# Transposes of q, k and x on TensorE, or by DMA between SBUF tiles: attention with a window and sinks, then an MLP, on one core

## The chip, the cores and the metric

The kernel runs on one core of one Trainium2 chip. The core has five engines that run side by side and wait for each other through semaphores: PE (TensorE, matrix products; PEld is its loading of weights), DVE (VectorE), ACT (ScalarE), POOL (GpSimd) and SP (SyncE). SP issues DMAs only; POOL and ACT issue DMAs too. DMAs move data between device memory and SBUF, or within SBUF, on 16 DMA engines that all queues share. The metric is the time of one execution on the device in microseconds; lower is better. Profiled executions carry a trace of every instruction.

## What is computed

Attention over 4 batches and 8 heads, 768 tokens each, head size 64. A token sees the 4 first tokens of its sequence (sinks) and the 128 tokens up to itself (window). The result of all heads, 512 numbers for a token, goes through an MLP with 2048 hidden units.

```python
def _attn_ref(q, k, v, n_sink, window) -> np.ndarray:
    B, H, S, D = q.shape
    scale = 1.0 / np.sqrt(D)
    scores = scale * np.matmul(q, k.transpose(0, 1, 3, 2))
    ...
    is_sink = pos[None, :] < int(n_sink)
    rel = pos[:, None] - pos[None, :]
    in_window = (rel >= 0) & (rel < int(window))
    keep = is_sink | in_window
    scores = np.where(keep, scores, -1000000000.0)
    scores = scores - np.max(scores, axis=-1, keepdims=True)
    a = np.exp(scores)
    a = a / (np.sum(a, axis=-1, keepdims=True) + 1e-09)
    return np.matmul(a, v).astype(np.float32)

def _moe_ref(x, w_in, w_out) -> np.ndarray:
    h = x @ w_in
    g = h * (1.0 / (1.0 + np.exp(-1.702 * h)))
    return (g @ w_out).astype(np.float32)
```

Inputs and output are float32; inside, the kernel works on float16 with float32 sums.

## The kernel before

**Tiling.** The 3072 tokens (4 batches x 768) are cut into 12 blocks of 256, three to a batch; `k` is the block, `r` its place in the batch, `j` the half of 128 tokens. The 8 heads are handled as 4 pairs, `p`. A block goes through these steps:

- Load (`load`, `load_rounded`, lines 425 to 481): POOL issues DMAs that bring q and k of the block into `qk16` and v into `v16`, rounding to float16 on the way: four DMAs for q and k and four for v. Blocks 0 and 1 load q, k or both through SP and ACT in float32 and round on an engine (`load_cast`). `qk16` and `v16` are rings of four buffers, so the loads of block k+4 wait for the last reader of block k.
- Transpose q and k (`front`, line 550, for blocks 0 to 3; `halves_qk`, line 604, from block 4): the scores need the head dimension on the partitions. PE transposes through PSUM and DVE or ACT copies the result to `qkT` (ring of three). From block 4 these are 32 transposes of 64 x 128 (line 618), put in behind the score matmuls of pairs 2 and 3 of the block before, into two PSUM banks.
- Sinks (`front`, lines 572 to 595): at r = 0, the transposed keys of the 4 sink tokens go to `ks16`; at r = 1 and 2 a matmul gives the scores against them (line 585) and ACT their exponentials (`ats`). The values of the sinks go to `vs16` through small DMAs on SP (line 474).
- Scores (`scores`, line 695), their exponentials on ACT (line 724, `at`) and a multiplication with `mask` on DVE (lines 738 and 742).
- Attention times values (`back`, lines 770 and 775), then DVE divides by the sum: a reciprocal (line 790) and a product (line 792) that writes `xn`, with the tokens on the partitions (ring of three).
- Transpose x (`back`, line 803, for blocks 0 to 2 and 11; `halves_x`, line 642, for blocks 3 to 10): 16 transposes of 64 x 128 a block, put in behind the score matmuls of pairs 0 and 1 of the next block, then two copies to `xT` (ring of three).
- First layer (`mm1`, line 843): 16 groups of four matmuls of 128 x 128 by 256 columns, tanh on ACT (line 857), and a DVE instruction (line 859) that writes `gT`.
- Second layer (`mm2_seven`, line 920, for blocks 1 to 11): seven products of half-size matrices in place of eight, with sums on DVE (lines 890 and 947); results go to `osb`, and SP issues the output DMAs (line 996). Block 0 takes `mm2` (line 1021).

**Order of the tokens.** In `qk16`, `v16` and all that follows, the tokens of a block do not stand in their natural order but with even and odd tokens apart, which the loads arrange by their address patterns. `mask` is made for that order on POOL (line 335), the sinks are found at the matching places, and the outputs are written as `paired` rows, two DMAs for each half of a block (lines 993 to 998).

**Order of the work.** The order of the instructions on each engine is fixed when the program is built. `Plan` (line 55) receives operations with an engine, a duration, a latency, their dependencies and a due time (`prio`, from `nominal(k, slot)` with a period of 16.6 us for a block); it plays them through in time, one engine at a time, taking the operation that can start first, and among those that can start within 20 ns the one with the lowest `prio`. What it decides is the order; the chip's own times then decide the waits. A DMA is an operation with the issue's duration and the transfer's share of the DMA engines; its end adds a fixed time and a lag (line 176). PSUM is eight banks that an operation acquires and a later one releases; the score operations with transposes behind them acquire six (line 710).

```python
            elif isinstance(lat, tuple):
                dma_free = max(s + (2400 if e == "POOL" else 2000), dma_free) + lat[0]
                o.end = dma_free + (lag(dma_free) if o.kind != "out" else 500)
```

PE works on several blocks at once: between the attention of one block and its first layer stand the first and second layer of the blocks before it. SP's instructions are a queue of their own: an output DMA that waits for `osb` holds what stands behind it.

Of the kernel before, what the change touches and what calls it, by code (L numbers as in the profile page):

```python
# [10 lines left out]
FP16 = mybir.dt.float16  # L11
AF = mybir.ActivationFunctionType
ALU = mybir.AluOpType

P = 128
D = 64
# [188 lines left out]
def kernel(  # L205
# [28 lines left out]

    EARLY = {1: 4, 2: 5, 3: 0}
    HALVES_FROM, HALVES_X_FROM = 4, 3
    V1_BEHIND = None

    SPLIT_TO = 1
# [13 lines left out]

    ident = pool.tile([P, P], FP16, name="ident")
    mask = pool.tile([P, 4 * P], FP16, name="mask")
    bias = pool.tile([P, 4 * P], FP16, name="bias")
    dummy = pool.tile([P, 8], FP16, name="dummy")
    zero = pool.tile([P, P], FP16, name="zero")
# [30 lines left out]
    def f16(o, i=0):  # L289
        return bank[o.banks[i]][:, 0:256].bitcast(FP16)  # L290
# [47 lines left out]
    def keep_sinks():  # L338
# [8 lines left out]
    o_bias = op("DVE", 310, 420, lambda: nc.vector.tensor_scalar(  # L347
        out=bias, in0=mask, scalar1=-1.0, scalar2=-OUT, op0=ALU.add, op1=ALU.mult), [o_mask], prio=MASK_AT, kind="mask")

    def ones():  # L350
        for t in v16:
            nc.vector.memset(t[:, :, :, D : D + 1], 1.0)
# [68 lines left out]
    def load_rounded(k, es, war):  # L421

        b, r = divmod(k, R)
        t0 = r * TB
        prio = load_at(f"a{k}")
        c16 = qk16[k % RQ].rearrange("p (i e h d) -> p i e h d", i=2, e=2, h=H)
        n = 2 if k <= SPLIT_TO else 1
        for c in range(n):
            hs = slice(c * H // n, (c + 1) * H // n)
            for e in es:  # L430
                src = (q, k_ap)[e]
                for i in range(2):
                    def f(e=e, i=i, hs=hs, src=src):
                        nc.gpsimd.dma_start(  # L434
                            c16[:, i, e, hs], src[b, hs, t0 : t0 + TB].rearrange("h (p i) d -> i p h d", i=2)[i]
                        )
                    o = op("POOL", ISSUE if n > 1 else ISSUE + 190, (QK_NS / n,), f, war,
                           prio=prio + 0.1 * c + 0.02 * (2 * e + i), kind="load")
                    loads.append(o)
                    for p in range(c * NP // n, (c + 1) * NP // n):  # L440
                        o_cqk.setdefault((k, p), []).append(o)

    def load(k):
        b, r = divmod(k, R)
        t0 = r * TB
        war = reuse("qk16", k % RQ)
        if k < max(ROUNDED_FROM):
            load_cast(k, [e for e in range(2) if k < ROUNDED_FROM[e]], war)
        load_rounded(k, [e for e in range(2) if k >= ROUNDED_FROM[e]], war)
        w16 = v16[k % RV]  # L450

        war = reuse("v16", k % RV) + ([o_ks[0, V1_BEHIND]] if k == 1 and V1_BEHIND is not None else [])

        o_cv[k] = []
        for j in range(2):
            for i in range(2):
                src = v[b, :, t0 + P * j : t0 + P * j + P].rearrange("h (a i) d -> i a h d", i=2)[i]
                o = op("POOL", ISSUE, (430 if k < 2 else V_NS,), lambda i=i, j=j, src=src: nc.gpsimd.dma_start(  # L458
                    w16[64 * i : 64 * i + 64, j, :, 0:D], src), war + [o_ones],
                       prio=load_at(f"v{k}"), kind="load")  # L460
                if not loads:
                    o.behind = o_mask0
                loads.append(o)
                o_cv[k].append(o)
        if r == 0:

            o_vs[b] = []
            for t in range(2):
                for i in range(2):
                    to = vs16[64 * t + 32 * i : 64 * t + 32 * i + 2, b, :, i]  # L470
                    fr = w16[64 * t : 64 * t + 2, 0, i::2, 0:E]
                    deps = [o_cv[k][t], o_vs0[b]]
                    if b:
                        o = op("SP", 450, (20,), lambda to=to, fr=fr: nc.sync.dma_start(to, fr), deps,
                               prio=nominal(k - 1, 0), kind="vs")
                    else:

                        o = plan.any(pick({"POOL": (400, 500), "DVE": (220, 320), "ACT": (420, 540)}, VS_ON),
                                     lambda eng, to=to, fr=fr: copy(eng, to, fr), deps, prio=VS_AT, kind="ks")
                    o_vs[b].append(o)  # L480
                    uses("v16", k % RV, o)
# [59 lines left out]
    def front(k, p):  # L541
# [5 lines left out]
        T = qkT[k % RKT]  # L547
        c16 = qk16[k % RQ].rearrange("p (i e h d) -> p i e h d", i=2, e=2, h=H)

        if k < HALVES_FROM:  # L550
            def tp():
                ps = f16(o_tp).rearrange("d (e j i p) -> d e j i p", e=2, j=2, i=2)
                for i in range(2):
                    for e in range(2):
                        nc.tensor.transpose(  # L555
                            ps[:, e, :, i, :], c16[:, i, e, 2 * p : 2 * p + 2].rearrange("s h d -> s (h d)"), ident
                        )

            if p == 0:
                o_T["war", k] = reuse("qkT", k % RKT)  # L560
            war = o_T["war", k]
            o_tp = op("PE", 4 * pe_ns(P), 3 * pe_ns(P) + P / 2.4 + 166, tp,
                      [*o_cqk[k, p], o_ident] + war, prio=base - 5 * h8, acq=("t", 1), kind="tp")
            uses("qk16", k % RQ, o_tp)
            o_tps[k, p] = o_tp
            o_cp = plan.any(pick({"DVE": (331, 430), "ACT": (477, 600)}, COPY[k]), lambda e: copy(
                e, T[:, :, :, p].rearrange("d j e s -> d e j s"),
                f16(o_tp).rearrange("d (e j s) -> d e j s", e=2, j=2)),
                [o_tp] + war, prio=base - 5 * h8, rel=[(o_tp, 0)], kind="cp")
            o_qkT[k, p] = [o_cp]  # L570
        As = ats[u % RA]
        if r == 0:
            def ks(eng):
                for i in range(2):
                    d = slice(64 * i, 64 * i + 64)
                    copy(
                        eng, ks16[d, NP * b + p].rearrange("d (i a) -> d i a", i=2)[:, :, 32 * i : 32 * i + 2],
                        T[d, 0, 1, p].rearrange("d (i a) -> d i a", i=2)[:, :, 0:2],
                    )
# [21 lines left out]

    SLOT = 30

    def halves_qk(k):


        T = qkT[k % RKT]
        c16 = qk16[k % RQ].rearrange("p (i e h d) -> p i e h d", i=2, e=2, h=H)
        war = reuse("qkT", k % RKT)

        def tp(ps):
            ps = [x.rearrange("d (e n i a) -> d e n i a", e=2, n=NP, i=2) for x in ps]
# [44 lines left out]
    def scores(k, pairs, more=None):  # L657
# [59 lines left out]
        for n, p in enumerate(pairs):  # L717
# [14 lines left out]
            if add:  # L732
                continue

            def m(A=A, m_=mask):
                if r:
                    a_ = A.rearrange("p i (n c) -> p (i n) c", c=2 * P)
                    nc.vector.tensor_tensor(  # L738
                        out=a_, in0=a_, in1=m_[:, 2 * P :].unsqueeze(1).to_broadcast((P, 4, 2 * P)), op=ALU.mult,
                    )  # L740
                else:
                    nc.vector.tensor_tensor(
                        out=A[:, :, 0:W], in0=A[:, :, 0:W],
                        in1=m_[:, 0:W].unsqueeze(1).to_broadcast((P, 2, W)), op=ALU.mult,
                    )

            o_m[k, p] = [op("DVE", 2 * W / 1.92 + 65, 2 * W / 1.92 + 155, m, o_e + [o_mask],
                           prio=base - 2 * h8, kind="mask")]

    def back(k, p):  # L750
# [35 lines left out]
        if r:  # L786
# [7 lines left out]
            in1=rc.to_broadcast((P, 2, 2, D)), op=ALU.mult),  # L794
            [o_r] + o_xT["warn", k], prio=base - 1.2 * h8, rel=[(o_a, 0)], kind="xn")
        o_n.setdefault(k, []).append(o_nn)
        if HALVES_X_FROM <= k < NK - 1:
            return

# [7 lines left out]
        uses("xn", k % RXN, o_x)  # L807

        def cx(e):
            to, fr = xT[k % RX][:, p], f16(o_x)[:, 0:TB]  # L810
            if k == NK - 1:

                to = to.rearrange("d (j a h) -> d j a h", j=2, h=2)
                fr = fr.rearrange("d (j h a) -> d j a h", j=2, h=2)
            copy(e, to, fr)
# [64 lines left out]
    def mm2_seven(k):  # L880
# [110 lines left out]
        for j, after in ((1, [r21, r22]), (0, [r11, r12])):  # L991
            rows = out[k * TB + j * P : k * TB + j * P + P, :]
            paired = rows.rearrange("(p i) f -> i p f", i=2)
            for i in range(2):
                def f(to=paired[i], fr=T[j][64 * i : 64 * i + 64], i=i):
                    nc.sync.dma_start(to, fr)
                o_d = op("SP", 500, (400.0,), f, after, prio=prio, kind="out")
                uses("osb", O[j], o_d)

    def mm2(k):  # L1000
# [55 lines left out]
    for k_ in range(NK):  # L1056
# [8 lines left out]
        if k_ < PAIRED_FROM:  # L1065
            for p_ in range(NP):
                scores(k_, (p_,))
        else:
            scores(k_, (0, 1), halves_x(k_ - 1) if k_ > HALVES_X_FROM else None)
            scores(k_, (2, 3), halves_qk(k_ + 1) if HALVES_FROM <= k_ + 1 < NK else None)  # L1070
        for p_ in range(NP):
            back(k_, p_)
        if k_ >= 1:
# [56 lines left out]
```

## Time and profile before

| | |
|---|---|
| median of 3 runs | 218.37 us (217.8 to 218.85) |
| span of the profiled execution | 216.2 us |
| PE, DVE, ACT, POOL busy | 210.8, 185.4, 133.1, 86.0 us |
| first layer on PE (line 843) | 768 matmuls, 103.7 us busy |
| second layer on PE (line 920) | 616 matmuls |
| transposes of q and k from block 4 (line 618) | 256 matmuls, 5.0 us busy |
| transposes of x, blocks 3 to 10 (line 642) | 128 matmuls, 3.2 us busy |
| copies to qkT, 1024 wide | 8 on ACT, mean 1032 ns; 8 on DVE, mean 683 ns |
| copies to xT, 512 wide | 16 on DVE, mean 416 ns |
| DMA | 21.41 MB in 79734 packets, 68184 of them under 512 bytes |

Busy time is the time in which at least one instruction of the group runs; matmuls overlap, so a group's mean duration is longer than the distance from one to the next. The DMA engines are nearly full for the first third of the span and work in bursts afterwards, as this row of 40 slices shows (each digit is tenths of a slice):

```profile
DMA  6999999999999498099970099091040031022042
```

### The profile page before, as it was taken

The page shows a single profiled execution, that of the slowest core. Times are in us where ns is not written, and L with a number is a line of the kernel's source. Part 1 is how long each engine was busy: PE and PEld are TensorE (multiplying, and loading weights), DVE is VectorE, ACT ScalarE, POOL GpSimd, SP SyncE. Part 2 cuts the span into 40 slices and gives each one's busy share as a digit, 9 for nine tenths or more (in the row PEclk, how much of TensorE's full clock was granted, in tenths as well). Part 3 has the DMA queues.
Part 4 walks back from the last instruction along what each step waited for, and adds up shares of the span by engine and source line. Part 5 has one row for each costly group of instructions (what it writes and reads, how often), then busy time and mean ns, then how long its engine had stood idle before and what let it go on. Part 6 is the DMA issues. An engine that isn't in the chain of part 4 may idle for free.

```text
span 216.2 us, 6592 instructions
## 1 busy us (share of the span) xinstructions
PE 210.8 (97%) x2680; PEld 181.0 (84%) x2680; DVE 185.4 (86%) x429; ACT 133.1 (62%) x277; POOL 86.0 (40%) x136
## 2 busy tenths in 40 slices
PE   7899999999999999999999999999999999999994
PEld 7568887678888988988888988888889889888883
DVE  5698899998988988988988979889979879878674
ACT  3867695366686775765675775864675865744330
POOL 7979564499996260699300080540000000000000
PEclk9999999999999999999999999999999999999999
DMA  6999999999999498099970099091040031022042
GB/s 179 215 196 179 200 192 205 168 163 166 108 167 165 30 144 77 5 133 170 89 124 3 0 96 125 5 114 36 3 97 3 0 76 28 0 52 49 2 100 97
DMA packets 79734, 21.41 MB, mean 99 GB/s; under 512 B 68184, under 2 KB 76888, under 8 KB 79704
## 3 DMA queue, kind: packets, MB, share of 16 engines
q0 software_dynamic: 71200, 12.59, 73.2%
q1 hardware_dynamic: 7416, 7.88, 13.5%
q10 hardware_dynamic: 1088, 0.52, 0.8%
q8 instruction: 21, 0.34, 0.7%
q14 instruction: 9, 0.07, 0.1%
HBM read 27.26 MB, written 6.29 MB: 155 GB/s over the span
## 4 chain that ended last, share of the span: by engine, by line
PE 92%; DVE 3%; DMA 2%; ACTq 1%; issue 0%
PE bank L843 39%; PE bank L920 31%; PE bank L695 5%; PE bank L775 5%; PE bank L1021 3%; DMA qk<-in_k_dram 2%; PE bank L618 2%; PE bank L770 2%; PE bank L585 2%; PE bank L555 1%; DVE osb L947 1%; PE bank L642 1%; PE bank L803 1%; ACTq L505 1%; PE bank L678 1%; DVE xn L792 1%
## 5 line engine op out<-in xcount | busy, mean ns | idle before, releaser
L843 PE MATMUL bank<-xT,w_in 128*128 128x256 f16 x768 | 103.7, 273 | 0.0
L857 ACT ACTIVATE th<-bank 128x512 f16<-128x512 f32 x96 | 57.6, 604 | 57.9 <-PE bank L843 51.6
L843 PEld LDWEIGHTS <-w_in 128*128 128x128 f16 x768 | 71.9, 98 | 8.9
L859 DVE SCALAR_TENSOR_TENSOR gT<-th,bank 128x512 f16<-128x512 f16 x96 | 64.9, 678 | 10.1 <-ACT th L857 9.8
L724 ACT ACTIVATE at<-bank 128x512 f16<-128x512 f32 (+1 forms) x96 | 49.1, 584 | 1.5 <-PE bank L695 1.1
L458 POOL DMA_DIRECT2D v<-in_v_dram x48 | 33.2, 719 | 30.4 <-PE bank L775 24.8
L920 PEld LDWEIGHTS <-sm 128*128 128x128 f16 x352 | 33.3, 98 | 4.2 <-issue 0.2
L920 PE MATMUL bank<-wt,sm 128*128 128x256 f16 x264 | 36.1, 273 | 0.0
L947 DVE SCALAR_TENSOR_TENSOR osb<-bank,osb 128x256 f32<-128x256 f32 x58 | 23.9, 417 | 11.8 <-PE bank L920 11.8
L920 PEld LDWEIGHTS <-gT 128*128 128x128 f16 x264 | 25.5, 98 | 3.4
L920 PE MATMUL bank<-w_out,gT 128*128 128x256 f16 x176 | 26.1, 273 | 0.0
L738 DVE TENSOR_TENSOR at<-at,mask 128x1024 f16<-128x1024 f16 x30 | 20.5, 683 | 0.2 <-ACT at L724 0.2
L792 DVE TENSOR_TENSOR xn<-bank,rcp 128x256 f16<-128x256 f32 x48 | 20.0, 417 | 0.6
L775 PE MATMUL bank<-v,at 128*128 128x65 f16 x352 | 20.0, 193 | 0.0
L434 POOL DMA_DIRECT2D qk<-in_q_dram x20 | 18.0, 925 | 0.6 <-DMA qk<-in_q_dram 0.5
L434 POOL DMA_DIRECT2D qk<-in_k_dram x20 | 18.0, 923 | 0.7 <-PE bank L843 0.5
L775 PEld LDWEIGHTS <-at 128*128 128x128 f16 x352 | 17.4, 97 | 0.9
L305 POOL COPY ks<-qkT 64x4 f16<-64x4 f16 x26 | 8.1, 313 | 18.6 <-DVE qkT L305 17.6
L890 DVE TENSOR_TENSOR sm<-gT 128x1024 f16<-128x1024 f16 x22 | 15.0, 680 | 0.1
L593 ACT ACTIVATE ats<-bank 128x256 f16<-128x256 f32 x32 | 13.0, 405 | 1.7 <-PE bank L585 1.6
L945 ACT ACTIVATE osb<-bank 128x256 f32<-128x256 f32 x22 | 8.4, 382 | 9.1 <-PE bank L920 9.1
L695 PE MATMUL bank<-qkT 64*128 64x256 f16 x192 | 13.3, 244 | 0.0
(58 smaller groups left out, 224.0 us busy)
## 6 DMA issues: line engine op xcount, KB each, us to landing
out_dram<-osb SPq DMA_DIRECT2D x48, 128.0 KB
v<-in_v_dram POOLq DMA_DIRECT2D x48, 64.0 KB, 5.1
qk<-in_q_dram POOLq DMA_DIRECT2D x20, 128.0 KB, 5.4
qk<-in_k_dram POOLq DMA_DIRECT2D x20, 128.0 KB, 5.6
w_out<-in_moe_w_out_dram POOLq DMA_DIRECT2D x4, 512.0 KB, 11.3
w_in<-in_moe_w_in_dram POOLq DMA_DIRECT2D x4, 256.0 KB, 6.6
w_in<-in_moe_w_in_dram POOLq DMA_DIRECT2D x2, 512.0 KB, 8.9
qk<-in_k_dram ACTq DMA_DIRECT2D x4, 128.0 KB
```

What stands on the lines that cost most here:

```text
L434: nc.gpsimd.dma_start(c16[:, i, e, hs], src[b, hs, t0 : t0 + TB].rearrange("h (p i) d -> i p h d", i=2)[i])
L458: o = op("POOL", ISSUE, (430 if k < 2 else V_NS,), lambda i=i, j=j, src=src: nc.gpsimd.dma_start(w16[64 * i : 64 * i + 64, j, :, 0:D], src ...
L695: nc.tensor.matmul(f32(o_b or o_s, 2 * n + i)[:, c : c + w].rearrange("s (j t) -> s j t", t=P), src[d, j, 1, p], T[d, j0:j1, 0, p], start= ...
L724: nc.scalar.activation(out=A[:, i, 0:W], in_=f32(o_b or o_s, 2 * n + i)[:, 0:W], func=AF.Exp, scale=scale)
L738: nc.vector.tensor_tensor(out=a_, in0=a_, in1=m_[:, 2 * P :].unsqueeze(1).to_broadcast((P, 4, 2 * P)), op=ALU.mult,)
L775: nc.tensor.matmul(avp()[:, j, i], A[:, i, c : c + P], src[:, jj, 2 * p + i, 0:E], start=not r and n == 0, stop=n == len(blocks) - 1, skip ...
L792: o_nn = op("DVE", 333, 425, lambda: nc.vector.tensor_tensor(out=X[:, p].rearrange("s j (h d) -> s j h d", h=2), in0=avp()[:, :, :, 0:D], ...
L843: nc.tensor.matmul(f32(holder[0])[:, bass.ts(e, TB)], w_in16[:, c, bass.ts(Fi, P)], X[:, c], start=(c == 0 and not (halved and e)), stop=( ...
L857: o_t = op("ACT", 477, 600, lambda first=first: nc.scalar.activation(out=th[first.places[0]], in_=f32(first), func=AF.Tanh, scale=0.851), ...
L859: o_g[k, s] = op("DVE", 595, 690, lambda first=first, s=s: nc.vector.scalar_tensor_tensor(out=g[:, 2 * s : 2 * s + 2].rearrange("p a t -> ...
L920: nc.tensor.matmul(f32(holder[bank_of])[:, 0:HM], x[:, Fi], w[:, Fi], start=first and Fi == 0, stop=Fi == NH - 1, skip_group_check=True)
L947: f, ns = (lambda: nc.vector.scalar_tensor_tensor(out=out, in0=src(), scalar=0.5, in1=add, op0=ALU.mult, op1=ALU.add)), (333, 425)
```

## The change

From block 3 on (`NATURAL = R`, the first block of the second batch) the tokens keep their natural order. q, k and v are then loaded with plain rows: still four DMAs of q and k for a block, but split by the half `j` and by q or k, and two DMAs of v in place of four. A second mask, `mask2`, is made for the natural order; sink keys and sink values are four tokens in a row, and the values take two small DMAs in place of four; the outputs are one DMA for each half in place of two.

The transposes of q and k of blocks 4 to 11 and of x of blocks 3 to 10 leave PE. SP issues them as DMAs that transpose between SBUF tiles: two for q and k of a block, from `qk16` to `qkT`, and one for x, from `xn` to `xT`, each with 128 partitions of 1024 half-precision numbers on either side. The copies from PSUM go with them. In the plan such a DMA has an issue time of 700 ns and a transfer of 1300 ns. The transposes of q and k are due seven slots before the block's period, that of x at the time at which the copies of x were due. The x of a block is transposed when its last pair's product (line 792) is there, in one piece for all four pairs.

The diff, cut to its core:

```diff
+    NATURAL = R
+    DMA_QK, DMA_X = 4, 3
+    T_SP, T_NS = 700, 1300
...
+    def make_mask2():
+        m = mask2.rearrange("s (g u t) -> s u g t", g=2, u=2)
+        for u, keep, sign in ((0, ALU.is_ge, 1), (1, ALU.is_gt, -1)):
+            nc.gpsimd.affine_select(out=m[:, u], in_=m[:, u], compare_op=keep, fill=0.0, base=0,
+                                    pattern=[[0, 2], [sign, P]], channel_multiplier=-sign)
+    MASK2_AT = 20000.0
+    o_m21 = op("DVE", 490, 550, lambda: nc.vector.memset(mask2, 1.0), prio=MASK2_AT, kind="const")
+    o_m20 = op("POOL", 900, 950, make_mask2, [o_m21], prio=MASK2_AT, kind="const")
+    o_mask2 = op("DVE", 300, 400, lambda: nc.vector.memset(mask2[0:n_sink, 0 : 2 * P], 1.0), [o_m20], prio=MASK2_AT,
+                 kind="const")
...
+        if k >= NATURAL:
+            cn = qk16[k % RQ].rearrange("p (j e h d) -> p j e h d", j=2, e=2, h=H)
+            for j in range(2):
+                for e in es:
+                    def f(e=e, j=j, src=(q, k_ap)[e]):
+                        nc.gpsimd.dma_start(
+                            cn[:, j, e], src[b, :, t0 + P * j : t0 + P * j + P].rearrange("h p d -> p h d"))
+                    o = op("POOL", ISSUE + 190, (QK_NS,), f, war, prio=prio + 0.02 * (2 * j + e), kind="load")
...
+        for j in range(2 if k >= NATURAL else 0):
+            src = v[b, :, t0 + P * j : t0 + P * j + P].rearrange("h p d -> p h d")
+            o = op("POOL", ISSUE + 100, (2 * V_NS,), lambda j=j, src=src: nc.gpsimd.dma_start(w16[:, j, :, 0:D], src),
+                   war + [o_ones], prio=load_at(f"v{k}"), kind="load")
...
+        if k >= max(DMA_QK, NATURAL) and p == 0:
+            transposed_qk(k)
+        if k < HALVES_FROM and k < max(DMA_QK, NATURAL):
...
+    def transposed_qk(k):
+        war = reuse("qkT", k % RKT)
+        cn = qk16[k % RQ].rearrange("p (j c) -> p j c", j=2)
+        done = []
+        for j in range(2):
+            def f(j=j):
+                nc.sync.dma_start_transpose(
+                    qkT[k % RKT][:, j].rearrange("d e n s -> d (e n) s"), cn[:, j])
+            o = op("SP", T_SP, (T_NS,), f, o_cqk[k, "j", j] + war, prio=nominal(k - 1, -7), kind="T")
+            uses("qk16", k % RQ, o)
+            done.append(o)
+        for p in range(NP):
+            o_qkT[k, p] = done
+
+    def transposed_x(k):
+        X = xn[k % RXN]
+        o = op("SP", T_SP, (T_NS,), lambda: nc.sync.dma_start_transpose(
+            xT[k % RX].rearrange("d n (j s) -> d (n j) s", j=2), X.rearrange("s n j d -> s (n j d)")),
+               [*o_n[k], *o_xT["war", k]], prio=nominal(k, 0) - 0.8 * L / 8, kind="T")
+        uses("xn", k % RXN, o)
+        for p in range(NP):
+            o_xT[k, p] = [o]
...
-            def m(A=A, m_=mask):
+            def m(A=A, m_=mask2 if k >= NATURAL else mask):
...
+        if DMA_X <= k < NK - 1:
+            if p == NP - 1:
+                transposed_x(k)
+            return
...
-            for i in range(2):
-                def f(to=paired[i], fr=T[j][64 * i : 64 * i + 64], i=i):
+            moves = [(paired[i], T[j][64 * i : 64 * i + 64]) for i in range(2)] if k < NATURAL else [(rows, T[j])]
+            for to, fr in moves:
...
-            scores(k_, (0, 1), halves_x(k_ - 1) if k_ > HALVES_X_FROM else None)
-            scores(k_, (2, 3), halves_qk(k_ + 1) if HALVES_FROM <= k_ + 1 < NK else None)
+            scores(k_, (0, 1), halves_x(k_ - 1) if HALVES_X_FROM < k_ <= DMA_X else None)
+            scores(k_, (2, 3), halves_qk(k_ + 1) if HALVES_FROM <= k_ + 1 < min(NK, DMA_QK) else None)
```

More of the change, by code (lines that the diff above doesn't have):

```diff
@@ L255 @@
     mask = pool.tile([P, 4 * P], FP16, name="mask")
+    mask2 = pool.tile([P, 4 * P], FP16, name="mask2")
     bias = pool.tile([P, 4 * P], FP16, name="bias")
@@ L427, in load_rounded @@
         n = 2 if k <= SPLIT_TO else 1
+        if k >= NATURAL:
[6 more added lines that the diff above has]
+                    o = op("POOL", ISSUE + 190, (QK_NS,), f, war, prio=prio + 0.02 * (2 * j + e), kind="load")
+                    loads.append(o)
+                    o_cqk.setdefault((k, "j", j), []).append(o)
+            for p in range(NP):
+                o_cqk[k, p] = o_cqk[k, "j", 0] + o_cqk[k, "j", 1]
+            return
         for c in range(n):
@@ L454, in load @@
         o_cv[k] = []
-        for j in range(2):
+        for j in range(2 if k >= NATURAL else 0):
+            src = v[b, :, t0 + P * j : t0 + P * j + P].rearrange("h p d -> p h d")
+            o = op("POOL", ISSUE + 100, (2 * V_NS,), lambda j=j, src=src: nc.gpsimd.dma_start(w16[:, j, :, 0:D], src),
+                   war + [o_ones], prio=load_at(f"v{k}"), kind="load")
+            loads.append(o)
+            o_cv[k].append(o)
+        for j in range(0 if k >= NATURAL else 2):
             for i in range(2):
@@ L467, in load @@
             o_vs[b] = []
-            for t in range(2):
+            for i in range(2 if k >= NATURAL else 0):
+                o = op("SP", 450, (20,), lambda i=i: nc.sync.dma_start(
+                    vs16[32 * i : 32 * i + n_sink, b, :, i], w16[0:n_sink, 0, i::2, 0:E]), [o_cv[k][0], o_vs0[b]],
+                       prio=nominal(k - 1, 0), kind="vs")
+                o_vs[b].append(o)
+                uses("v16", k % RV, o)
+            for t in range(0 if k >= NATURAL else 2):
                 for i in range(2):
@@ L548, in front @@
         c16 = qk16[k % RQ].rearrange("p (i e h d) -> p i e h d", i=2, e=2, h=H)
-        if k < HALVES_FROM:
+        if k >= max(DMA_QK, NATURAL) and p == 0:
+            transposed_qk(k)
+        if k < HALVES_FROM and k < max(DMA_QK, NATURAL):
             def tp():
                 ps = f16(o_tp).rearrange("d (e j i p) -> d e j i p", e=2, j=2, i=2)
+                if k >= NATURAL:
+                    cn = qk16[k % RQ].rearrange("p (j e n s) -> p j e n s", j=2, e=2, n=NP)
+                    for j in range(2):
+                        for e in range(2):
+                            nc.tensor.transpose(ps[:, e, j].rearrange("d i p -> d (i p)"), cn[:, j, e, p], ident)
+                    return
                 for i in range(2):
@@ L575, in ks @@
                     d = slice(64 * i, 64 * i + 64)
+                    if k >= NATURAL:
+                        copy(eng, ks16[d, NP * b + p, 32 * i : 32 * i + n_sink], T[d, 0, 1, p, 0:n_sink])
+                        continue
                     copy(
@@ L602 @@
     SLOT = 30
+    def transposed_qk(k):
+        war = reuse("qkT", k % RKT)
+        cn = qk16[k % RQ].rearrange("p (j c) -> p j c", j=2)
+        done = []
+        for j in range(2):
+            def f(j=j):
[12 more added lines that the diff above has]
+        uses("xn", k % RXN, o)
+        for p in range(NP):
+            o_xT[k, p] = [o]
     def halves_qk(k):
@@ L609, in halves_qk, with tpn, copiesn @@
         war = reuse("qkT", k % RKT)
+        if k >= NATURAL:
+            cn = qk16[k % RQ].rearrange("p (g s) -> p g s", s=P)
+            def tpn(ps):
+                for g in range(4 * NP):
+                    for h in range(2):
+                        d = slice(64 * h, 64 * h + 64)
+                        nc.tensor.transpose(ps[h][:, 64 * g : 64 * g + 64], cn[d, g], ident[d, d])
+            def copiesn(o, b0, base):
+                uses("qk16", k % RQ, o)
+                done = [plan.any(pick({"DVE": (598, 690), "ACT": (903, 1030)}, COPY[k]), lambda e, h=h: copy(
+                    e, T.rearrange("d j e n (h a) -> d h (j e n) a", h=2)[:, h],
+                    f16s(o, b0 + h).rearrange("d (g a) -> d g a", a=64)), [o] + war,
+                    prio=base - 5 * L / 8, rel=[(o, b0 + h)], kind="cp") for h in range(2)]
+                for p in range(NP):
+                    o_qkT[k, p] = done
+            return tpn, copiesn, 4 * NP * SLOT, [x for p in range(NP) for x in o_cqk[k, p]] + war
         def tp(ps):
@@ L745, in m @@
                     )
-            o_m[k, p] = [op("DVE", 2 * W / 1.92 + 65, 2 * W / 1.92 + 155, m, o_e + [o_mask],
+            o_m[k, p] = [op("DVE", 2 * W / 1.92 + 65, 2 * W / 1.92 + 155, m, o_e + [o_mask2 if k >= NATURAL else o_mask],
                            prio=base - 2 * h8, kind="mask")]
@@ L796, in back @@
         o_n.setdefault(k, []).append(o_nn)
+        if DMA_X <= k < NK - 1:
+            if p == NP - 1:
+                transposed_x(k)
+            return
         if HALVES_X_FROM <= k < NK - 1:
@@ L809, in cx @@
         def cx(e):
[L810 to L815, printed above, removed]
+            copy(e, xT[k % RX][:, p], f16(o_x)[:, 0:TB])
         o_xT[k, p] = [plan.any(pick({"DVE": (205, 300), "ACT": (264, 380)}, COPY[k]), cx, [o_x],
@@ L993, in mm2_seven, with f @@
             paired = rows.rearrange("(p i) f -> i p f", i=2)
-            for i in range(2):
-                def f(to=paired[i], fr=T[j][64 * i : 64 * i + 64], i=i):
+            moves = [(paired[i], T[j][64 * i : 64 * i + 64]) for i in range(2)] if k < NATURAL else [(rows, T[j])]
+            for to, fr in moves:
+                def f(to=to, fr=fr):
                     nc.sync.dma_start(to, fr)
-                o_d = op("SP", 500, (400.0,), f, after, prio=prio, kind="out")
+                o_d = op("SP", 500, (800.0 / len(moves),), f, after, prio=prio, kind="out")
                 uses("osb", O[j], o_d)
```

## The prediction

> **What bounds the kernel now.** I read the busy times first, then the chain that ended last, then the waits, then one block of the PE timeline, then the DMA queues.
>
> ```profile
> span 216.2 us, 6592 instructions
> PE 210.8 (97%) x2680; PEld 181.0 (84%) x2680; DVE 185.4 (86%) x429; ACT 133.1 (62%) x277; POOL 86.0 (40%) x136
> ...
> PEclk9999999999999999999999999999999999999999
> ...
> q0 software_dynamic: 71200, 12.59, 73.2%
> q1 hardware_dynamic: 7416, 7.88, 13.5%
> ...
> PE 92%; DVE 3%; DMA 2%; ACTq 1%; issue 0%
> ```
> ```profile
> ACT th L857 <- PE bank L843: 51.6, 61, 2.0
> ```
> PE is busy 97% at full clock, and 92% of the chain is PE. The largest wait of all is ACT waiting for PE. The kernel is bound by what PE is given to do, from about 20 us to 207 us without a gap; DVE is second at 86%. So a PE instruction taken out is worth its issue time, as long as nothing new makes PE wait. The two transposes that the change takes out stand in the PE timeline of one block like this (start, duration):
>
> ```profile
> 118.63 0.33 PE L695 MATMUL bank<-qkT 64*128 64x256 f16 x4
> 118.80 0.63 PE L618 MATMUL bank<-ident,qk 64*128 64x64 f16 x32
> 119.36 1.05 PE L920 MATMUL bank<-wt,sm 128*128 128x256 f16 x8
> ...
> 126.97 0.40 PE L642 MATMUL bank<-ident,xn 64*128 64x64 f16 x16
> 127.30 1.05 PE L843 MATMUL bank<-xT,w_in 128*128 128x256 f16 x8
> ```
>
> **What it removes.** Per block, 32 transposes of q and k (L618, blocks 4 to 11) and 16 of x (L642, blocks 3 to 10). The chain gives the 32 as one piece of 0.47 us (14.7 ns each), so 16 cost 0.235. Eight blocks: 8 x (0.47 + 0.235) = 5.6 us off PE. From start to next start the two take 0.56 and 0.33, which would be 8 x 0.89 = 7.1 us, but part of that is the scores' tail, which stays. I take 5.6, bounds 5.6 and 7.1.
>
> The copies out of PSUM go too: 16 of qkT (8 on ACT at 1.03 us, 8 on DVE at 0.68) and 16 of xT on DVE at 0.42, together 8.3 us of ACT and 12.2 us of DVE. Both engines run beside PE, so I count this as nothing; it only makes room. The score groups ask for four PSUM banks instead of six; PE shows no idle time for banks before, so nothing again.
>
> **What it adds at the start.** A second mask: two affine selects on POOL (a quarter-size one on the old mask takes 0.42) ahead of the first v loads, and on DVE a memset of 0.49 and one of 0.27. POOL's first loads go out up to about 0.95 us later, but the DMA engines are then mostly busy with the q and k loads that SP and ACT issue. Between 0 and 0.95; I take 0.2.
>
> **What it adds in flight.** 24 DMAs from SP of 256 KB each, SBUF to SBUF, and the trace of before has no such transfer. What matters is the time L from SP's issue until PE may go on. Fixed part: the two output DMAs that SP issues at 157.81, on an otherwise idle DMA, move their first data 1.1 us later (slices of 0.125 us from 157.6):
>
> ```profile
> 157.81 1.11 SPq L996 DMA_DIRECT2D out_dram<-osb  x2
> ```
> ```profile
> DMA  0000000000479993999940000279957999661000
> ```
> A v load of 64 KB lands 3.0 us after issue in the quiet window 120 to 160; its 512 packets at 35.6 ns (73.2% of 16 x 216.2 us over 71200 packets) on 16 engines are 1.1 us, which leaves 1.9. So the fixed part is 1.1 to 1.9; I take 1.5. Moving the data, D: at the rate of SP's own queue (7.88 MB in 13.5% of 16 x 216.2 us, 270 GB/s over 16 engines) 256 KB take 0.97 us. As 1024 runs of 128 half-precision numbers, priced like the load queue's packets, 1024 x 35.6 ns / 16 = 2.3 us. It has the one's queue and the other's run length, so I take the middle, 1.6. L is then 3.1 us on a quiet DMA. While loads are under way, the v loads show how much is added: 5.1 us in the median over the whole run against 3.0, so +2.1, and L is 5.2.
>
> Against L stands the PE work between the end of x (xn) of pair 3 and the first L843 matmul that reads this block's xT. I count it in the changed kernel's PE order, from the last L775 matmul of pair 3: blocks 6 and 9 have 11 groups of four 256-wide matmuls (0.437 each), two sinks (0.11), one score group (0.55): 5.6 us. Blocks 7 and 10: one group more, 6.0. Blocks 5 and 8: 12 groups, two score groups, one attention group (0.36): 6.7. Block 4: 8.0; block 3: about 10.8. From this goes the time until xn is done:
>
> ```profile
> 133.35 0.29 PE L775 MATMUL bank<-v,at 128*128 128x65 f16 x4
> ```
> ```profile
> 133.84 0.17 DVE L790 RECIPROCAL rcp<-bank 128x4 f32<-128x4 f32 x1
> 133.94 0.66 DVE L859 SCALAR_TENSOR_TENSOR gT<-th,bank 128x512 f16<-128x512 f16 x1
> 134.51 0.42 DVE L792 TENSOR_TENSOR xn<-bank,rcp 128x256 f16<-128x256 f32 x1
> ```
> 133.64 to 134.93 is 1.3 us. Cover W: 4.3 (6, 9), 4.7 (7, 10), 5.4 (5, 8), 6.7 (4), 9.5 (3). Loads are issued near x of blocks 3, 4, 5, 7 and 8; blocks 6, 9 and 10 are quiet. With L = 3.1 and 5.2 only block 7 is late, by 0.5. With D = 2.3 and fixed part 1.9, L is 4.2 and 6.3: late 0.9 + 1.6 + 0.9 = 3.4. So 0 to 3.4; I take 0.5. What a late x delays is all of PE: its order is fixed, every later block's attention stands behind that matmul, and each block can lose again.
>
> q and k have more cover: from block 6 on the first score that reads them stands over 15 us of PE work behind the transposes. Only block 4 is tight: its last load was issued at 45.2 and such loads land 4.9 us later (median from 36 to 60 us), so at 50.1; its first sink matmul (L585) came at 58.0, and two transposes of 5.2 us, the second issued some 1 us after the first, fit in between with 1.7 us to spare. SP is one queue: a transpose of q and k that waits for a load holds the x transpose and the output DMAs behind it (block 5's first half stands ahead of x of block 3, which has 9.5 of cover). For this stage 0 to 1.5; I take 0.5. POOL refills a q/k buffer only when its transpose has landed, a few us later than before, with blocks of slack. POOL's v issues fall from four to two a block, output issues on SP from four to two: both beside PE, nothing.
>
> **Sum.** -5.6 + 0.2 + 0.5 + 0.5 = -4.4 us: a span of 211.8, and 218.37 - 4.4 = 214.0 us for the median (the profiled span lies 2.2 below the median of the runs). The bounds of the parts give 211.3 to 218.6.
>
> Beside this sum, which does not use it: the Trainium skill speaks against the change in "VectorE: DVE Perf Modes", The three transpose paths: a 128x128 transpose is 390 ns on TensorE and 1309 ns by DMA, and its rules say to use TensorE where a PSUM destination will do. By it, as an estimate and with the eight squares of a transfer in turn, D is 10.5 us and the time about 275. Its "Advanced Engine Details and Errata", X-Bar Transpose (TRN2), says the opposite, as fast as ordinary DMAs, 350 to 400 GB/s; an estimate from that is D of 0.7 and about 213.5. The trace has only the 270 GB/s of the ordinary queue, which is nearer the second.
>
> **Rivals.** (1) *The transfer goes square by square.* A 256 KB transpose is eight 128x128 squares; SP needs 0.63 us to issue one SBUF-to-SBUF DMA (vs<-v). If each square costs that in turn, D is 5.0, L 6.5 quiet and 8.6 loaded. Late: block 4 1.9, 5 3.2, 6 2.2, 7 3.9, 8 3.2, 9 2.2, 10 1.8: 18.4 us, and 218.4 - 5.6 + 0.7 + 18.4 = 231.9. It decides from D of about 3.0: there the delays (blocks 5 and 8 1.2, 7 1.9, 6 and 9 0.2) eat the gain. For it: no row shows that a transpose keeps the ordinary rate. (The skill's first page would hold by this mechanism, with a larger delay by its own figure.) Against: the packets' prices above. (2) *Gain and delay cancel*, D near 3, 218. (3) *DVE becomes the bound*: it was 86% busy. Against: it loses 12 us. Were half the gain lost, 215.6 to 216.5. (4) *Nothing in flight is late and the scores' tail shrinks*: 218.4 - 7.1 + 0.2 = 211.5. That the change does not do what it says is out: the changed order has 384 PE transposes fewer and 24 transposing DMAs on SP.
>
> **Chances.** Forecast with (3), 212.5 to 217, 0.52; (4) 0.05; (2) 0.10; (1) 0.33, spread from 219.5 to 232 and beyond. About 1.1 us (0.5%) is what a measurement of this kernel can tell from none. Faster 0.57, same 0.10, slower 0.33. The forecast's own range is 212 to 217; the range that holds 8 in 10 reaches into (1): 211.9 to 228.
>
> **What would show it.** No L618 or L642 on PE from block 4; SP rows of the transposes, and the time from their issue to the first L843 of the block. Right: PE stays at 97% and no wait of L843 on xT is over 1 us. Wrong: waits of L843 on DMA xT, one a block, near 2 us or more. If q and k are late instead, L585 or L695 waits for DMA qkT.

## The result, and the profile after

The changed kernel takes 222.07 us (median of 5 runs, 221.55 to 225.88) against 218.37 us (5 runs, 217.8 to 218.85): a ratio of 1.0168, 95% interval 1.0139 to 1.0196. It is slower by 3.7 us; forecast were 214.0, so 4.4 faster. The profiled execution of the changed kernel is the longest of its five (225.88 us, span 224.2, mean granted clock 0.983) and is left out of the ratio; the others have spans of 219.8 to 220.8 at a clock of 0.989 to 0.992, so what follows is read from a trace that is longer than usual.

The page after, with the lines that answer to those shown of before:

```profile
span 224.2 us, 5817 instructions
PE 209.4 (93%) x2297; PEld 175.6 (78%) x2297; DVE 177.9 (79%) x406; ACT 127.6 (57%) x271; POOL 77.0 (34%) x119
...
PEclk9999999999999999997699999999999999999999
DMA  5999999999999999999909029998022031011022
...
q0 software_dynamic: 70912, 12.59, 75.0%
q1 hardware_dynamic: 32504, 14.17, 33.1%
...
PE 75%; DMA 18%; POOL 2%; DVE 1%; ACTq 0%; ACT 0%; issue 0%
```

The change does what it says: 383 matmuls fewer in the trace of PE (384 by the program), and 24,800 more packets than before, about 1024 for each of the 24 transposing DMAs. But DMA, 2% of the chain before, is 18% now. Behind its first slice the row of the DMA engines is full without a gap up to 112 us (slices of 5.6 us), where before it had gaps from 70 us on. And PE loses clock in the last two of these slices, 101 to 112 us.

The waits view and the chain in order of time (start, us, what) say which transfers. The waits are engine, line, releaser: us in total, times, longest.

```profile
PE bank L942 <- DMA xT<-xn: 6.1, 2, 3.6
PE bank L640 <- DMA qkT<-qk: 2.0, 1, 2.0
```
```profile
52.63 11.28 DMA qkT<-qk
...
79.15 8.44 DMA xT<-xn
97.63 7.77 DMA xT<-xn
```

L942 is the first layer (L843 before) and L640 the sink matmul (L585 before). Three transposes are late: the second of q and k of block 4 takes 11.3 us from its issue until PE goes on, x of block 4 takes 8.4, x of block 5 7.8. PE waits 2.0 + 2.5 + 3.6 = 8.1 us for them. From block 6 on it waits for none.

On an idle DMA the same transfer is quick. SP issues x of block 9 at 165.49, and the row of the DMA engines (0.1 us a slice, from 165.4) starts 1.1 us later and stays full for about 1.2 us, at some 215 GB/s, before the output DMAs join:

```profile
165.49 1.24 SPq L677 DMA_TRANSPOSE xT<-xn  x1
```
```profile
DMA  0000000000001699999999999999989920009998
```

Where x lands while nothing else runs, the trace has 3.6 us from issue to landing. Beside loads, all transfers take longer, the loads too. The median to landing of the q loads (last number) goes from 5.4 in the kernel before to 6.4 with the natural order alone (`e1_natural`, below) and 8.9 with the change, so most of the rise comes with the transposes:

```profile
qk<-in_q_dram POOLq DMA_DIRECT2D x20, 128.0 KB, 5.4
```
```profile
qk<-in_q_dram POOLq DMA_DIRECT2D x20, 128.0 KB, 6.4
```
```profile
qk<-in_q_dram POOLq DMA_DIRECT2D x20, 128.0 KB, 8.9
```

That transposes issued by SP and loads issued by POOL slow each other agrees with the Trainium skill, "DMA: Bandwidth & Descriptors", Issuing engines are not separate DMA queues: DMAs of all issuing engines run on the same 16 engines and interleave. Around x of block 5, POOL issues eleven loads without a pause, from 95.52 to 105.15 us.

The transposes also stand in line on SP. In its timeline, the four transposes of blocks 7 and 8 hold it from 84.96, waiting for loads or for PE, and x of block 5, whose last product DVE finished at 96.87, follows them:

```profile
96.46 0.41 DVE L892 TENSOR_TENSOR xn<-bank,rcp 128x256 f16<-128x256 f32 x1
```
```profile
84.96 12.58 SPq L666 DMA_TRANSPOSE qkT<-qk  x4
97.63 1.88 SPq L677 DMA_TRANSPOSE xT<-xn  x1
```

But this line costs little at the issue: x of block 5 is issued 0.76 us after its product, x of block 4 (behind two `vs` DMAs) 0.69, and x of block 9, with SP free, 0.03. The 7.8 and 8.4 us begin only at the issue.

The wait for x of block 5 costs twice. Before it ends, the granted clock falls (windows: stretch, its length, busy time of PE, PEld, DVE, ACT and POOL, then the clock, DMA share and GB/s), and the 16 matmuls behind it take 3.60 us:

```profile
100.00:105.00 5.00, 1.83 (x26) 1.43 (x23) 3.38 (x7) 2.95 (x8) 5.00 (x6) 0.89 1.92 169
105.00:110.00 5.00, 4.55 (x22) 3.25 (x23) 1.58 (x3) 1.57 (x3) 0.15 (x1) 0.50 2.08 200
```
```profile
105.45 3.60 PE L942 MATMUL bank<-xT,w_in 128*128 128x256 f16 x16 [3.62 <-DMA xT<-xn]
```

At full clock the same 16 take 1.9. From 100 to 115 us the clock is 0.89, 0.50 and 0.93, which is 3.4 us lost; about 0.8 of it falls into the wait itself, so some 2.6 us are lost while PE works. The Trainium skill, "TensorE: Matmul & The Clock Gate", Why this matters for your kernels, says to leave no gap over about 3 us between matmuls. This wait of 3.62 agrees; one of 3.11 us in a later kernel (`e5_mask_late`) left the clock at 1.00. Here PE stopped at 101.83 and the clock was 1.00 up to 103.75 and 0.50 from 104.0 on, so it fell some 2.0 us into the wait, while the wait of 2.47 us for x of block 4 passed at full clock, so the traces show no length of a gap from which the clock falls.

Last, the start: the second mask goes ahead of the first loads on POOL, and those go out 0.9 us later (3.69 before). Everything behind it shifts; the first layer of block 1 starts at 28.4 us in place of 27.4 (the last two lines: before, after).

```profile
3.81 0.82 POOL L360 TENSOR_SCALAR_AFFINE_SELECT mask<-mask 128x256 f16<-128x256 f16 x2
4.58 2.94 POOL L496 DMA_DIRECT2D v<-in_v_dram  x4
```
```profile
27.38 0.60 PE L843 MATMUL bank<-xT,w_in 128*128 128x256 f16 x4
```
```profile
28.37 0.61 PE L942 MATMUL bank<-xT,w_in 128*128 128x256 f16 x4
```

The account of the two profiled spans: -5.6 for the transposes, +1.0 for the start, +8.1 for the three waits, +0.6 for small new waits of PE on ACT and DVE, +2.6 for the clock: 6.7 of the 8.0 us. The rest is not accounted for.

### The profile page after: what moved, and what is told of

It is laid out like the page before. It is cut to its first block, busy times and chain, and to the rows that moved or that the text cites. A ratio compares the mean times of both kernels' runs of the same rounds, so it can differ in the third digit from the quotient of the medians.

```text
span 224.2 us, 5817 instructions
## 1 busy us (share of the span) xinstructions
PE 209.4 (93%) x2297; PEld 175.6 (78%) x2297; DVE 177.9 (79%) x406; ACT 127.6 (57%) x271; POOL 77.0 (34%) x119
## 4 chain that ended last, share of the span: by engine, by line
PE 75%; DMA 18%; POOL 2%; DVE 1%; ACTq 0%; ACT 0%; issue 0%
PE bank L942 35%; PE bank L1019 26%; DMA xT<-xn 7%; DMA qkT<-qk 5%; PE bank L875 4%; PE bank L795 4%; DMA w_in<-in_moe_w_in_dram 3%; PE bank L1121 3%; DMA qk<-in_k_dram 2%; PE bank L870 1%; PE bank L640 1%; POOL v L496 1%; DVE osb L1046 1%; POOL w_in L413 1%; PE bank L907 1%; ACTq L549 0%
## 5 line engine op out<-in xcount | busy, mean ns | idle before, releaser
L942 PE MATMUL bank<-xT,w_in 128*128 128x256 f16 x768 | 101.4, 276 | 6.8 <-DMA xT<-xn 6.1
L942 PEld LDWEIGHTS <-w_in 128*128 128x128 f16 x768 | 73.3, 99 | 18.9 <-DMA xT<-xn 6.6
L1019 PE MATMUL bank<-wt,sm 128*128 128x256 f16 x264 | 36.9, 275 | 0.0
L489 POOL DMA_DIRECT2D v<-in_v_dram x18 | 15.9, 886 | 54.5 <-PE bank L875 44.3
L1019 PEld LDWEIGHTS <-gT 128*128 128x128 f16 x264 | 25.0, 99 | 4.4 <-issue 1.1
L1019 PE MATMUL bank<-w_out,gT 128*128 128x256 f16 x176 | 25.6, 276 | 0.2 <-ACT osb L1044 0.2
L452 POOL DMA_DIRECT2D qk<-in_k_dram x18 | 16.2, 897 | 4.7 <-DMA qk<-in_k_dram 1.7
L452 POOL DMA_DIRECT2D qk<-in_q_dram x18 | 16.0, 892 | 3.7 <-DVE wt L972 1.9
L1019 PE MATMUL bank<-wt,gT 128*128 128x256 f16 x88 | 13.1, 273 | 0.4 <-DVE osb L1046 0.4
L1019 PE MATMUL bank<-w_out,sm 128*128 128x256 f16 x88 | 13.0, 273 | 0.0
```

The source lines that it names most:

```text
L452: nc.gpsimd.dma_start(cn[:, j, e], src[b, :, t0 + P * j : t0 + P * j + P].rearrange("h p d -> p h d"))
L489: o = op("POOL", ISSUE + 100, (2 * V_NS,), lambda j=j, src=src: nc.gpsimd.dma_start(w16[:, j, :, 0:D], src), war + [o_ones], prio=load_at( ...
L942: nc.tensor.matmul(f32(holder[0])[:, bass.ts(e, TB)], w_in16[:, c, bass.ts(Fi, P)], X[:, c], start=(c == 0 and not (halved and e)), stop=( ...
L1019: nc.tensor.matmul(f32(holder[bank_of])[:, 0:HM], x[:, Fi], w[:, Fi], start=first and Fi == 0, stop=Fi == NH - 1, skip_group_check=True)
```

## The experiments

The theory: the transposes themselves are cheap, and the loss comes from transposing while the loads fill the DMA engines, plus the second mask at the start. In its first form (theory A of the first four kernels) it also blamed the queue on SP. Since the plan is made anew for each kernel, the order of the instructions also moves a little in each.

### Natural order alone (e1_natural)

```diff
-    DMA_QK, DMA_X = 4, 3
+    DMA_QK, DMA_X = NK, NK - 1
```


> All transposes stay on PE; what is left of the change is the natural order of the tokens, the second mask at the start, and fewer, larger DMAs. Theory A (the loss comes from transposing DMAs that crawl and queue behind each other on SP while the loads fill the DMA engines, plus about 1.2 us from the second mask standing ahead of the first loads): 218.4 + 1.2 = 219.6 us, no PE wait for a DMA of xT or qkT. Rival B (the natural order itself costs the time): 221 to 222 us. Rival C (the transposing DMAs are the whole loss): 218.4 us.

219.8 us, ratio 1.0084 (1.0059 to 1.0108). As theory A said (219.6). PE waits for no xT or qkT, and the first layer of block 1 starts at 28.7 us in place of 27.4; that 1.3 us is still there at the last matmul of the first layer (208.0 against 206.7). So natural order with its second mask costs about 1.8 us (ratio 1.0084), and by subtraction the DMA transposes, with what they save, the other 2.

### q and k only (e2_qk_only), x only (e3_x_only)

q and k only:

```diff
-    DMA_QK, DMA_X = 4, 3
+    DMA_QK, DMA_X = 4, NK - 1
```
x only:

```diff
-    DMA_QK, DMA_X = 4, 3
+    DMA_QK, DMA_X = NK, 3
```


> q and k by DMA from block 4, x on PE. Theory A: the transposes of q and k still crawl but only block 4 has no cover for that, so one PE stall of about 2 us before the first sink matmul of block 4, no other; 32 x 8 PE transposes fewer (3.8 us): 218.4 + 1.2 - 3.8 + 2.0 = 217.8 us. Rival D (transposes of q and k are late everywhere): 221 us or more, with waits of L640 or L795 for qkT in several blocks.

> x by DMA from block 3, q and k on PE. Theory A (x is late because it stands behind transposes of q and k in SP's queue): without those, x of blocks 3 to 5 lands within 5 us of its issue, PE waits under 1 us in all: 218.4 + 1.2 - 1.9 = 217.7 us. Rival E (the loads alone make x late, whatever else SP has): issue to landing stays near 8 us for blocks 4 and 5, stalls of 2 us and more there, and 221 us or more.

q and k only: ratio 0.9965 (0.9938 to 0.9991), which is 217.4 us against 218.2; the median of all ten runs is 218.16 (216.75 to 220.46). Theory A (217.8) is within 0.4 of either. In its profile q and k take 8.7 us in the median to land, and PE waits 0.3 us for them in all: they crawl, and it hardly matters, since they have cover.

x only: 224.61 us in the profiled run (span 222.9), the shortest of four; the others take 228.32 to 230.0, and no ratio was formed. Theory A in its first form, that x is late because it stands behind q and k, has fallen. Of rival E the direction holds, x is late without them and the time is over 221; its sizes do not. It named 8 us and waits of 2 us and more in blocks 4 and 5; PE waits for x of blocks 3, 5, 7 and 8, 3.9 us in all and 1.7 at the longest, and not for block 4. From issue until PE goes on these four take:

```profile
59.46 6.92 DMA xT<-xn
...
93.67 6.14 DMA xT<-xn
...
129.17 5.22 DMA xT<-xn
...
146.30 5.45 DMA xT<-xn
```

PE also waits 2.3 us for ACT's reads of PSUM in the new order. Why the other three take longer still stays open.

### DMA transposes from block 6 on (e4_late)

```diff
-    DMA_QK, DMA_X = 4, 3
+    DMA_QK, DMA_X = 6, 6
```


> DMA transposes from block 6 on only, for q and k and for x; blocks 3 to 5 on PE. Theory A: no transposing DMA stands between an early block and its reader, so PE waits for none; 6 x 32 and 5 x 16 PE transposes fewer (4.0 us): 218.4 + 1.2 - 4.0 = 215.6 us. Rival F (a transposing DMA costs as much as it saves, wherever it is): 218 us or more.

216.15 us, ratio 0.9918 (0.9883 to 0.9953): faster than before, 3.65 us less than natural order alone, for a saving of 4.0 on PE. PE waits for no transpose at all. The q and k of block 6 are transposed into full engines from 66.7 us on, with cover; x of block 6 is issued at 108.6, when the DMA row has been empty for over 2 us, and x takes 4.4 to land from there on. So here a transposing DMA is worth its saving where it has much cover or meets no loads.

### The mask made late (e5_mask_late), and both (e6_mask_late_dma_late)

```diff
+    o_m20.behind = o_w[7]
     for a_, b_ in zip(loads, loads[1:]):
```
The second kernel has beside it:

```diff
-    DMA_QK, DMA_X = 4, 3
+    DMA_QK, DMA_X = 6, 6
```


> The changed kernel, with the second mask made on POOL after the last load of the weights instead of ahead of the first loads. Theory A (the mask pushes all early loads back, and PE's first layer with them): the first load of v goes out near 3.7 us again, PE is back in step with before by 30 us, 222.1 - 1.6 = 220.5 us, the waits for xT and qkT stay. Rival G (the other early differences, such as fewer and larger DMAs, are the cause of the late start): 222 us.

> The mask late and DMA transposes from block 6 on only, for q and k and for x. Theory A: both losses gone, 4.0 us of PE transposes saved: 216.2 - 1.7 = 214.4 us, no PE wait for xT or qkT. Rival G: 216.2 us.

With the mask late the first load goes out at 3.69 us again and the first layer of block 1 starts at 27.5 us. But alone it brings 221.66 us, ratio 1.0176 (1.0113 to 1.0239), not to be told from the change: PE still waits 5.5 us for x in blocks 4 and 5, and for block 4, which now comes earlier, 3.11 in place of 2.47:

```profile
85.78 1.05 PE L942 MATMUL bank<-xT,w_in 128*128 128x256 f16 x8 [3.11 <-DMA xT<-xn]
```

With transposes from block 6: 215.76 us, ratio 0.9864 (0.9817 to 0.9912), against 216.15 and 0.9918; the profile keeps 1.7 us of it up to the last matmul of the first layer (203.0 against 204.7), the medians show 0.4 and the ratios 1.2, and their intervals overlap. So the mask's price is shown in the traces (1 to 1.7 us) and not settled in the times.

### The loads held while x is on its way (e7_x_only_loads_held)

x only, with one more instruction on POOL: it copies one number of block k - 3's xT into the buffer that block k's loads then overwrite, so these wait until that x has landed.

```diff
-    DMA_QK, DMA_X = 4, 3
+    DMA_QK, DMA_X = NK, 3
...
+        if k - 3 >= DMA_X:
+            go = op("POOL", 80, 180, lambda: nc.gpsimd.tensor_copy(
+                out=qk16[k % RQ][0:1, 0:1], in_=xT[(k - 3) % RX][0:1, 0, 0:1]), war + o_xT[k - 3, 0],
+                prio=load_at(f"a{k}") - 0.2, kind="go")
+            uses("xT", (k - 3) % RX, go)
+            loads.append(go)
+            war = [go]
```


> x by DMA from block 3, q and k on PE, and the loads of block k (6 and later) held until x of block k - 3 has landed, so that no load is asked for while an x is on its way. Theory H (loads that share the DMA engines make x late): issue to landing of x falls from 4.7 us in the median to under 4.0 in blocks 4 to 10, PE waits for xT under 0.5 us in all instead of 3.9: 219.0 us span and 221 us, and less spread between runs. Rival I (the transfer alone is longer than its cover): landing and waits as without the hold, span 222.9 us. Rival J (the held loads come too late for their own readers): new PE waits for q, k or v, over 223 us.

218.27 us, ratio 0.9987 (0.9964 to 1.0009), in place of 224.61 and more, and the ten runs lie within 1.7 us of each other. Theory H holds, and by more than it said. The view of xT, of the kernel with x only and then with the hold:

```profile
DMA to landing us min/median/max: 3.1/4.7/6.1
```
```profile
DMA to landing us min/median/max: 3.0/3.1/3.9
```

No wait of PE for xT is left. The same transfers, on the same queue, land 1.6 us earlier in the median once no loads are asked for beside them, and the q loads themselves land in 4.2 us in the median in place of 7.2; rival I (too long for its cover anyway) and J (loads too late) fall.

### All of the change, mask late, loads held (e9_all_loads_held); block 4 on PE (e10_from5_loads_held)

Both have the late mask and the hold of the kernel before this one in the text:

```diff
+    o_m20.behind = o_w[7]
...
+        if k - 3 >= DMA_X:
...
+            war = [go]
```
The first leaves the two starts at 4 and 3; the second has beside it:

```diff
-    DMA_QK, DMA_X = 4, 3
+    DMA_QK, DMA_X = 5, 3
```


> All transposes of the change by DMA (q and k from block 4, x from block 3), the mask late, and the loads of block k (6 and later) held until x of block k - 3 has landed. It differs from the kernel with only the mask late (221.7 us) by the hold alone. Theory H (loads that share the DMA engines with the transposes are the loss): no PE wait for xT over 0.5 us, full saving of 5.6 us less up to 1 us for block 4: 213 to 214.5 us. Rival L (x is late because it stands behind transposes of q and k in SP's queue, whatever the loads do): x of blocks 4 and 5 still lands 6 us or more after its issue, PE waits of 2 us and more, 218 us or above.

> As with all transposes by DMA, the mask late and the loads held, but q and k of block 4 on PE. Theory H: block 4's wait cannot occur, 0.5 us of PE work comes back: within 0.7 us of the kernel with all of them, and nearer 213.7 us if that one waits for qkT of block 4. Rival L: as there, 218 us or above.

All held: 215.27 us, ratio 0.9859 (0.9835 to 0.9884). It differs from the kernel with the mask late (221.66) by the hold alone, which is 6.4 us. The longest wait of PE for a transpose is 0.3 us:

```profile
PE bank L949 <- DMA xT<-xn: 0.3, 1, 0.3
```

Rival L falls as it was put: with the loads held, PE goes on 3.8 us after the issue of x of block 4, though the transposes of block 6 were issued 4.8 and 3.0 us ahead of it. But the DMA row is nearly empty from 75.4 us until x is issued at 75.99, so their data had moved by then. What the hold doesn't separate is sharing from standing in line, since loads that come later also bring the transposes of q and k later. That both play a part is likely and not shown: x of block 5 took 7.8 us in the change and 6.1 with no q and k on SP, in kernels whose order differs.

With block 4's q and k on PE: 214.17 us, ratio 0.9807 (0.9793 to 0.9822), 1.1 us less, more than the 0.7 expected, and the runs agree within 0.2 us. Where the 1.1 comes from is not shown, since PE waited for no qkT of block 4 in the first either.

### From block 5 and block 6, mask late (e8_mask_late_5_6)

```diff
+    o_m20.behind = o_w[7]
-    DMA_QK, DMA_X = 4, 3
+    DMA_QK, DMA_X = 5, 6
```


> As with the mask late and DMA transposes from block 6, but q and k by DMA from block 5. Theory A: block 5's transposes have some 3 us to spare by the order and do not stand ahead of an x, so 0.5 us more is saved: 213.9 us. Rival K: they crawl beside the loads of blocks 6 and 7, and PE waits for qkT of block 5 by 1 us or more: 215 us or above.

214.31 us, ratio 0.9816 (0.978 to 0.9851), as theory A said; PE waits for no transpose. This and the kernel before it are the fastest here, and not to be told apart: one keeps x on PE while the DMA is full, the other keeps the loads off the DMA while x moves.

## Why the prediction was wrong

**Right: what is saved, and the quiet transfer.** The kernel was bound by PE and gives back most of what PE is spared where nothing is late: 3.65 us of 4.0 with transposes from block 6, against natural order alone. The all-DMA kernel with held loads is 3.1 us under before for 5.6 spared, with block 4 on PE 4.2 for 5.2, both with the late mask. The fixed part of 1.1 us to the first data is what the trace shows, the data took 1.2 us against 1.6 taken (bounds 0.97 and 2.3), and L on a quiet DMA was 3.1 to 3.6 against 3.1 (4.4 with transposes from block 6 on). The cover W was about right too: 6.7 and 5.0 us in blocks 4 and 5, counted as 6.7 and 5.4. Where L had its quiet size, the longest wait was 0.3.

**Wrong: "While loads are under way ... +2.1, and L is 5.2".** This is the step that failed, in size: L was 8.4 and 7.8 for x of blocks 4 and 5, and the waits for x, taken as 0.5 us within 0 to 3.4, were 6.1. The sign that the prediction had named came, waits of the first layer on xT over 2 us, though in two blocks only. The 2.1 was the loads' own delay in the kernel before, whose DMA was full only part of the time. It was carried over as a constant, although the change itself fills the same engines: the median of the q loads went from 5.4 to 8.9, and with these 3.5 us added, L would have been 8.7 by an estimate from the result. That loads beside it are what makes x late is shown by holding them: with x alone by DMA it then lands in 3.0 to 3.9 us in place of 3.1 to 6.1, and with the whole change and the late mask PE waits 0.3 us for x in place of 5.5. Smaller, and also left out, are the 0.7 us that x of blocks 4 and 5 waits for its turn on SP; the prediction named that queue for x of block 3, and not the four transposes of blocks 7 and 8 ahead of x of block 5.

**Wrong: block 4, "0 to 1.5; I take 0.5".** Measured 2.0: from the issue of the second transpose until PE goes on it was 11.3 us, where 5.2 was taken, again with the DMA engines full. With q and k only, the same transfer took 9.8 and PE waited 0.3.

**Mis-sized: the start, 0.2 within 0 to 0.95.** Measured 1.0 to 1.3. The argument that the DMA engines are busy then anyway did not hold: POOL's first loads go out 0.9 us later, the first of w_in behind them 1.5 later (11.92 against 10.38), and the first layer starts 1.0 later.

**Left out: the clock.** A late x was priced at its wait. The wait of 3.62 us cost some 2.6 us more in clock; by their mean clock, the other four executions lost an estimated 1.8 to 2.4 us. The four terms, x, block 4, start and clock, measured 6.1, 2.0, 1.0 and 2.6 where 0.5, 0.5, 0.2 and nothing were taken: 10.5 of the 12.4 us between the forecast span of 211.8 and the profiled one.

**The rivals.** The time came out on the side of (1), between its point of decision and its price, but not by its mechanism: a transfer doesn't go square by square. Its eight squares take 1.2 us of data, not 5. The same row decides between the two rules of the Trainium skill that were weighed there: the 1309 ns of "VectorE: DVE Perf Modes", The three transpose paths, don't add up over eight squares, and the 350 to 400 GB/s of "Advanced Engine Details and Errata", X-Bar Transpose (TRN2), are more than the 215 seen. Rival (2), gain and delay cancel, rested on D near 3; D was 1.2, and the delay came from L beside loads. Rival (4), nothing late, falls with the three waits. Rival (3), DVE as the bound, found nothing: DVE is busy less than before.

## What to carry to other kernels

Before work is moved from a full engine to DMA, read the row of the DMA engines by stage, and add the change's own transfers to it before pricing a transfer's latency. Here, x with 4 to 7 us of cover did not bear sharing the engines with loads that nobody needed yet, while q and k with much cover did. Holding such loads back, or starting the scheme some blocks later, together with a late mask, turned 3.7 us of loss into some 4 us of gain. On a queue that issues in order, a transfer with little cover can also lose some of it to those ahead of it, 0.7 us here.

## What the runs showed of the hardware that was not expected

A transposing DMA of 256 KB between SBUF tiles occupies SP for 1.23 us when quiet, and up to 5.3 us when the engines are full (x of block 3, right behind three others); that SP then waits for room is likely and not shown. Its data move at about 215 GB/s, less than the 350 GB/s and more that the output DMAs behind it show in the same window. And PE's granted clock was 0.50 from 2.0 us into a wait of 3.62 us until about 5 us behind it, but stayed at 1.00 through one of 3.11.
